# Attention and top-1 experts on one core: the second products of full blocks read the weights in place, at addresses in 16 registers of TensorE, and routing is staged two groups ahead

## The chip, the cores and the metric

One Trainium2 chip, one core of it. The number is the device time of one execution in microseconds (us). The kernel before has run three times: 1196.02, 1198.91 and 1199.16 us, median 1198.91. All inputs lie in HBM when the time starts, and the output has to lie there when it ends.

## The reference, cut

```python
# B, N, C = 4, 5056, 256;  experts E = 8, width F = 1024
qn = q / (norm(q, axis=1) + 1e-06)                  # a norm for each channel, over the tokens
kn = k / (norm(k, axis=1) + 1e-06)
a  = softmax(kn.transpose(0, 2, 1) @ qn / tau)      # 256 x 256 for each batch
x  = (v @ a).reshape(B * N, C)                      # 20224 tokens
logits = x @ w_gate
e, gate = argmax(logits), its softmax probability
out[token] = gate * (relu(x[token] @ w1[e]) @ w2[e])
```

## The kernel before, in words

**Attention.** A batch has 10 groups of 512 tokens (`T` = 4 tiles of 128). SyncE loads the inputs as 128x1024 tiles (`fed`), three ahead of their use (`AHEAD`). For a batch, TensorE multiplies k and q tiles (`sp`, line 226), the softmax gives the matrix `a` (kept as a high and a low half, `a_h` and `a_l`), and `px` (line 396) is v times `a`, together with the router's logits. ScalarE casts each v tile to `hi` (line 192), VectorE makes the remainder `lo` (line 194), and ScalarE also squares and sums tiles by channel for the norms (line 184). ScalarE does its instructions in program order.

**Routing.** For each token VectorE finds the expert and a slot behind the tokens of that expert. ScalarE and VectorE pack the row (`rows`, lines 352 and 353: the token as two float16 parts, its gate factor, its number), and GpSimd writes it to its slot in the DRAM tensor `xs` with an indirect DMA (line 523).

**Experts in blocks.** A block is 256 rows of one expert, read from `xs` by SyncE with a transposing DMA (`xT`, line 699). The float16 parts are multiplied as high*high + high*low + low*high. A full block has 48 products of 128x128x256 for the first matrix (`hp`, line 730) and 48 for the second (`y`, line 756). ScalarE's ReLU (line 738) and VectorE (line 739) make the two halves of the hidden layer, `ht`. All experts' weights stand in SBUF in `W`, 8192 columns of float16 for each expert, but which expert a block has is known only on the chip: VectorE reads the number into a register (line 711) and copies the weights in eight pieces of 128x1024 to buffers `wp` (line 718, `piece`), four for the first matrix and four for the second; `WP` = 5 buffers. TensorE reads only `wp`. ScalarE scales `y` to `o` (line 766), and GpSimd scatters it to `out` (line 769).

**Lists of blocks.** Experts can start on a batch's rows before the last batch is routed. After certain numbers of tokens (`SORTED`) `table(stage)` counts on the chip which 256-row blocks must by now be full, and writes their experts and first rows into a list `c_tb`; SyncE (line 694) and VectorE (line 711) read an entry for each block. `SURE` is the number of full blocks that any data must have by then: 5, 12, 32, 52 and 72. What is left is done in small blocks of 128 rows, 18 of them here, at half the products of a full block. A block's load waits for all scatters of its stage and of those before (`loaded`).

**Order.** The attention of batches 1 to 3 is a side stream, given out between the blocks: `marks` and `amounts` say how much of it (in rough ns of TensorE) must have been issued by which block, linearly in between. A list `coming` sets the order of the loads of `fed`. The batch's list is made behind its tenth group. `EARLY` = 2 ends a batch's side work two blocks ahead of the first block that needs it. A scheduler then orders each engine's instructions by their dependencies and priorities.

Of the kernel before, what the change touches and what calls it, by code (L numbers as in the profile page):

```python
# [20 lines left out]
P = 128  # L21
# [7 lines left out]
G = 10  # L29
# [3 lines left out]
SORTED = [CUT * T * P] + [N * (b + 1) for b in range(B)]  # L33
# [31 lines left out]
def attention_then_experts(ctx, tc, qk, v, wt, chs, kc, out):  # L65
# [97 lines left out]
    WP = 5  # L163
    PT = 2 * T
    EARLY = 2
    PAUSE = -1
# [67 lines left out]
    def rest_of(b, sp, x_split):  # L234
# [107 lines left out]
        pending, packed, slots_of = [], [], {}  # L342

# [13 lines left out]
        def give(g):  # L357
            rows = packed.pop(0)
            z, si = slots_of.pop(g)
            vec.reciprocal(out=rows[:, :, 256], in_=z)  # L360
            for t in range(T):
                n = 64 if g == G - 1 and t == T - 1 else P
                held.append((
                    0 if b == 0 and g < CUT else b + 1, rows, t, si[:, t : t + 1], b * N + (g * T + t) * P, n, b == 0
                ))

        for pair in range(G // 2):
# [5 lines left out]
            for h in range(2):  # L373
                g = 2 * pair + h
                if b == 0:
                    raw = v_cell(g)
                else:
                    raw = fed("v", b, g)
                if x_split:
                    hl = split(raw)  # L380
                xg = work.tile([P, T, C + E], F32, tag="xg", name="xg", bufs=2)
                for t in range(T):
                    if b > 0:
                        px = ps_a.tile([P, C + E], F32, tag=f"p{t % 2}", name="px")
# [30 lines left out]
                if b == 0 or h == 1 or pair > 0:  # L415
                    convert()
                if h == 0 and b > 0 and pair > 0:
# [16 lines left out]
            last = pair == G // 2 - 1  # L434
            if last:
                vec.memset(ex[64:P, :, PT], 0.0)
# [26 lines left out]
            if b == 0 or last:  # L463
# [5 lines left out]
        drip(False, len(held))  # L469
# [60 lines left out]

    written = [[] for _ in range(LAST + 1)]
    SYNC = mybir.DependencyInfo(mybir.DependencyClass.Sync, mybir.DependencyReason.DATA)

    def scattered(stage, ins):
        raw = ins.ins
        for s2 in range(LAST):
# [6 lines left out]
    def loaded(stage, ins):  # L543
# [3 lines left out]
        for s2 in range(stage + 1, LAST):  # L547
# [5 lines left out]
    def padded(ins):  # L553
        raw = ins.ins
        for s2 in range(LAST):
# [20 lines left out]

    def table(stage):
# [6 lines left out]
        whole = work.tile([1, 512], F32, tag=tag, name="c_grid", bufs=bufs)  # L584
        grid = whole[:, 0 : 2 * 24 * E].rearrange("p (a i e) -> p a i e", a=2, e=E)
        square = whole[:, 384:448].rearrange("p (a e) -> p a e", e=E)
# [65 lines left out]
        te_f = tiny.tile([1, 24], F32, name="c_ef", bufs=1)[:, 0:quota]  # L652
        ts_f = tiny.tile([1, 24], F32, name="c_sf", bufs=1)[:, 0:quota]
# [3 lines left out]
        tb = tiny.tile([1, 2, 24], I32, name="c_tb", bufs=3)  # L657
# [5 lines left out]
        if final:  # L663
# [3 lines left out]
            gap = tiny.tile([1, 24], F32, name="c_gap", bufs=1)[:, 0:quota]  # L667
# [24 lines left out]
    def block_load(stage, tab, i):  # L692
        nt = P if stage == LAST else BLK
# [13 lines left out]
    def block(stage, tab, i, xT, mt):  # L707
# [12 lines left out]

        hts = []
        for f in range(8):
# [12 lines left out]
            behind[0] = mm.ins.name  # L735
            if f % nf == nf - 1:
# [98 lines left out]
    vec.tensor_scalar(out=before[0][:, :, 0], in0=e7, scalar1=NPAD / P, scalar2=None, op0=ALU.mult)  # L835
    done = one.tile([1, E], F32, name="done")
# [65 lines left out]
    left, soon = [("k", 2, n) for n in range(half)], list(range(20))  # L902
    steps = 0
    for r in range(1, E):
        for _ in range(6):
            steps += 1
            if steps % 4 == 3 and left:
                coming.append(left.pop(0))
            if steps >= 33:
                coming.append(("c", 2, soon.pop(0)))  # L910
        coming += [("c", 1, n) for n in range(2 * r + 4, 2 * r + 6)]
# [28 lines left out]
    def opening():  # L940
        scores_of(2)
        steps = 0
        for r in range(1, E):
            for _ in range(6):
# [3 lines left out]
                if steps % 4 == 3 and steps < 4 * HALF:  # L948
                    yield next(chunks[2])
                if steps >= 33:  # L950
                    yield next(norms_of[2])
# [4 lines left out]
            take(norms, 2)  # L956

    def rows_of(b):
        at = 0
        for n in rests[b]:  # L960
            yield n
# [9 lines left out]
        tables[b + 1] = yield from table(b + 1)  # L971
        if b == B - 1:
            tables[LAST] = yield from table(LAST)
# [8 lines left out]
    parts = [42 * 1000 + HALF * CHUNK + 10 * 300, 5000 + X_ALL + HALF * CHUNK + 10 * 300]  # L982
    parts += [5000 + X_ALL + nch * CHUNK + 20 * 300, 5000 + X_ALL]
    marks = [0.0, float(SURE[0])] + [SURE[b] - EARLY for b in range(1, B)]
# [70 lines left out]
```

## Time and profile before

| | |
|---|---|
| median of the runs shown | 1198.91 us |
| the profiled execution's own time | 1198.22 us |
| its span in the trace | 1196.4 us |
| TensorE matrix products, busy | 1162.0 us |
| TensorE weight loads, busy (beside the products) | 1026.0 us |
| VectorE / ScalarE / GpSimd, busy | 807.1 / 618.4 / 458.8 us |
| DMA, mean over the span | 148 GB/s |

The span runs from the first to the last instruction; 1.8 us of the execution's own time lie outside it. "Busy" counts an engine's computing instructions only. Each engine also has a sequencer, which takes the instructions in order, and does register work and waits by itself; the views mark its rows with a q (SPq, DVEq, PEldq). A product on TensorE has a weight load ahead of it, which has rows of its own (PEld).

### The profile page before, as it was taken

The numbers are of one execution on the slowest core, as the hardware profiler recorded it, in microseconds if no ns is written. First come the engines' busy times: TensorE is split into PE (matmuls) and PEld (weight loads), VectorE is DVE, ScalarE is ACT, GpSimd is POOL, SyncE is SP. The second block draws the span as 40 slices with busy tenths as digits, with TensorE's granted clock in tenths as the row PEclk, the third lists the DMA queues.
The fourth block names the chain that finished last, engine by engine and source line by source line (L and its number), as shares of the span: only waits on it lengthen the run. The fifth ranks groups of instructions, "written<-read, shape, count | busy, mean of one in ns | idle before, by whom it ended". The sixth has DMA issues, their size and how long they took to land. (4 is left out here: it accounts for less than half of the span.)

```text
span 1196.4 us, 28325 instructions
## 1 busy us (share of the span) xinstructions
PE 1162.0 (97%) x10194; PEld 1026.0 (86%) x10194; DVE 807.1 (67%) x2122; ACT 618.4 (52%) x1385; POOL 458.8 (38%) x724
## 2 busy tenths in 40 slices
PE   9998999899899999999999999999999999999998
PEld 7777879688778888998888988999878888889997
DVE  5575787776686776667687666767665555556886
ACT  6586478697745665666644555555422333223332
POOL 0067812228481343433545145363552222222222
PEclk9999999999899999999999999999999999999999
DMA  9968998958625555565644233222142211211121
GB/s 376 410 259 289 335 379 244 285 180 260 193 92 136 157 163 160 164 174 168 153 118 101 74 83 97 83 76 67 59 119 54 55 50 50 54 44 46 51 50 23
DMA packets 153488, 177.38 MB, mean 148 GB/s; under 512 B 116604, under 2 KB 118017, under 8 KB 151424
## 3 DMA queue, kind: packets, MB, share of 16 engines
q1 hardware_dynamic: 137952, 133.94, 38.6%
q0 software_dynamic: 15392, 41.60, 9.4%
q8 instruction: 81, 1.33, 0.5%
q14 instruction: 63, 0.52, 0.1%
HBM read 111.49 MB, written 43.29 MB: 129 GB/s over the span
## 5 line engine op out<-in xcount | busy, mean ns | idle before, releaser
L756 PE MATMUL y<-wp,ht 128*128 128x256 f16 x3888 | 454.6, 273 | 6.2 <-DVE wp L718 2.9
L730 PE MATMUL hp<-xT,wp 128*128 128x256 f16 (+1 forms) x4320 | 450.9, 262 | 1.6 <-DVE ht L739 1.0
L756 PEld LDWEIGHTS <-ht 128*128 128x128 f16 x3888 | 372.4, 98 | 59.7 <-ACT ht L738 7.2
L730 PEld LDWEIGHTS <-wp 128*128 128x128 f16 x4320 | 383.6, 98 | 46.4 <-issue 2.6
L718 DVE COPY wp<-W 128x1024 f16 (+1 forms) x720 | 291.9, 440 | 184.3 <-PE y L756 139.4
L769 POOL DMA_INDIRECT out<-o,mt x162 | 179.2, 1106 | 465.7 <-ACT o L766 442.1
L738 ACT ACTIVATE ht<-hp 128x512 f16<-128x512 f32 x324 | 192.3, 594 | 171.3 <-PE hp L730 169.5
L739 DVE SCALAR_TENSOR_TENSOR ht<-hp,ht 128x512 f16<-128x512 f32 x324 | 222.4, 687 | 44.3 <-ACT ht L738 41.9
L523 POOL DMA_INDIRECT xs<-rows,r_si x160 | 178.6, 1116 | 138.9 <-ACT rows L352 58.3
L766 ACT ACTIVATE o<-y,b_fac 128x256 f32<-128x256 f32 x162 | 68.8, 469 | 246.0 <-PE y L756 228.3
L513 POOL TENSOR_SCALAR rows<-kt 128x1 int32<-128x1 f32 x160 | 44.9, 281 | 127.0 <-PE sp L226 79.3
L398 ACT COPY xg<-px 128x264 f32<-128x264 f32 x160 | 57.8, 370 | 59.7 <-PE px L396 39.4
L352 ACT ACTIVATE rows<-xg,x_sc 128x256 f16<-128x256 f32 x160 | 71.2, 499 | 23.4 <-issue 8.1
L194 DVE TENSOR_TENSOR lo<-fed,hi 128x1024 fp32r<-128x1024 f32 x50 | 61.8, 1235 | 28.1 <-ACT hi L192 28.1
L353 DVE SCALAR_TENSOR_TENSOR rows<-xg,x_sc,rows 128x256 f16<-128x256 f32 x160 | 71.2, 480 | 13.4 <-ACT rows L352 13.0
L396 PE MATMUL px<-a_h,hi 128*128 128x264 f32 x240 | 73.9, 310 | 5.6 <-ACT hi L192 5.5
L396 PE MATMUL px<-a_h,lo 128*128 128x264 f32 x240 | 68.5, 292 | 0.0
L396 PE MATMUL px<-a_l,hi 128*128 128x264 f32 x240 | 68.5, 288 | 0.0
L400 ACT ACTIVATE xjunk<-xg 128x256 bf16<-128x256 f32 x160 | 66.8, 417 | 2.7
L192 ACT CAST hi<-fed 128x1024 fp32r<-128x1024 f32 x50 | 52.0, 1040 | 24.0 <-PE sp L226 13.2
L184 ACT ACTIVATE fed<-fed 128x1024 f32<-128x1024 f32 x54 | 56.7, 1050 | 13.7 <-DMA fed<-in_by_channel 13.7
L396 PEld LDWEIGHTS px<-a_h,hi 128*128 128x128 f32 x240 | 45.8, 192 | 8.4 <-ACT hi L192 6.9
(161 smaller groups left out, 973.2 us busy)
## 6 DMA issues: line engine op xcount, KB each, us to landing
fed<-in_by_channel SPq DMA_DIRECT2D x54, 512.0 KB, 4.1
fed<-in_qk SPq DMA_DIRECT2D x40, 512.0 KB, 4.6
W<-in_w SPq DMA_DIRECT2D x15, 1024.0 KB, 10.6
fed<-in_v SPq DMA_DIRECT2D x30, 512.0 KB, 4.5
raw<-in_qk SPq DMA_DIRECT2D x20, 512.0 KB, 9.2
W<-in_qk SPq DMA_DIRECT2D x20, 512.0 KB, 10.2
W<-in_v SPq DMA_DIRECT2D x10, 512.0 KB, 11.0
W<-in_by_channel SPq DMA_DIRECT2D x6, 512.0 KB, 10.2
```

Source lines behind the costliest of these rows:

```text
L352: act.activation(r16[:, t, 0:C], x, AF.Copy, scale=by)
L353: vec.scalar_tensor_tensor(out=r16[:, t, C : 2 * C], in0=x, scalar=by, in1=r16[:, t, 0:C], op0=ALU.mult, op1=ALU.subtract)
L396: mm = pe.matmul(px, hl[vh][:, c, ts], ah[:, c, :], start=(n == 0), stop=(n == 5))
L400: act.activation(junk, xg[:, t, 0:C], AF.Square, accum_out=ss[:, h * T + t : h * T + t + 1])
L523: ins = pool.indirect_dma_start(out=xs[:, :], out_offset=bass.IndirectOffsetOnAxis(ap=slot[:n], axis=0), in_=row[:n], in_offset=None)
L718: vec.tensor_copy(out=t, in_=Wf[:, ds(e * 8192 + n * 1024, 1024)])
L730: mm = pe.matmul(hp[:, f % nf, :], wp[:, dc, wh, (f % 2) * P : (f % 2 + 1) * P], xT[:, 2 * xh + dc, :], start=(n == 0), stop=(n == 5),)
L738: evicted.append(act.activation(ht[:, 0], hp, AF.Relu).ins.name)
L739: halved = vec.scalar_tensor_tensor(out=ht[:, 1], in0=hp, scalar=0.0, in1=ht[:, 0], op0=ALU.max, op1=ALU.subtract)
L756: mm = pe.matmul(ys[:, j, :], hts[f // nf][:, hh, f % nf, j * P : (j + 1) * P], wps[f // 2][:, f % 2, wh, :], start=(n == 0), stop=(n == 23),)
L766: act.activation(o, ys[:, j, :], AF.Copy, scale=fac[:, j : j + 1])
L769: ins = pool.indirect_dma_start(out=out[:, :], out_offset=bass.IndirectOffsetOnAxis(ap=mt.bitcast(I32)[:, j, 1:2], axis=0), in_=o, in_offs ...
```

## The change

- **Second products in place.** In all stages but the last (`straight`) the 48 `y` products of a block read `W` itself. VectorE computes 16 column addresses (`b_where`, line 740 of the changed kernel), one instruction on TensorE loads them into 16 registers (line 761), placed among the block's first products, and each `y` product (line 787) takes its address from one of them. The four copies for the second matrix are gone in these blocks; small blocks copy all eight as before. Over the program the copies go from 720 (90 blocks x 8) to 480 (68 x 4 + 26 x 8). `WP` is 4.
- **Stages two groups ahead.** A list is made behind group 8 of a batch's 10 (`TAIL` = 2, `ROUTED`); the last two groups' rows belong to the next stage. `SURE` becomes 5, 12, 28, 48 and 68 full blocks, and 26 small ones follow (94 blocks in place of 90). `EARLY` is 3, `marks` and `parts` follow, and scatters are no longer flushed at a batch's end.
- **Load order.** Three written lists (`opens`) say after which step of the opening a load and its work come, in place of rules.
- **Schedule.** The scheduler orders by estimated durations (`schedule_with_timeline_sim`).

```diff
-SORTED = [CUT * T * P] + [N * (b + 1) for b in range(B)]
+TAIL = 2
+SORTED = [CUT * T * P, N] + [N * b + (G - TAIL) * T * P for b in range(1, B)]
...
-    WP = 5
+    WP = 4
...
-    EARLY = 2
-    PAUSE = -1
+    EARLY = 3
+    TAKES = 6
+    GROUPS = [CUT, G - CUT, G - TAIL] + [G] * (B - 2) + [TAIL]
+    PAUSE, ROUTED = -1, -2
...
+            stage = int(g >= CUT) if b == 0 else b + 1 + (g >= G - TAIL)
...
+            if b > 0 and pair == (G - TAIL) // 2 - 1:
+                yield ROUTED
+        if b == 0:
+            drip(False, len(held))
-        drip(False, len(held))
...
+        straight = stage != LAST
+        if straight:
+            where = tiny.tile([1, 16], I32, name="b_where", bufs=2)
+            vec.scalar_tensor_tensor(
+                out=where, in0=tab[0][0:1, i : i + 1].to_broadcast([1, 16]), scalar=8192.0, in1=pieces_at,
+                op0=ALU.mult, op1=ALU.add,
+            )
...
+            if straight and f == 1:
+                (load,), at = nc.values_load_multi_w_load_instructions(
+                    where, engines=[ENG.PE], min_val=4096, max_val=8192 * (i + 1 if stage == 0 else E) - 256,
+                    skip_runtime_bounds_check_because=WHY, bass_reorder=False,
+                )
+                tc.add_manual_dep(load.ins, mm.ins.name, HERE, reason="among the first products")
...
-                if j == 0 and n < 16 and n % 4 == 0:
+                if not straight and n < 16 and n % 4 == 0:
                     wps.append(piece(4 + f // 2).rearrange("p (f s d) -> p f s d", f=2, s=2))
+                w2 = Wf[:, ds(at[2 * f + wh], C)] if straight else wps[f // 2][:, f % 2, wh, :]
                 mm = pe.matmul(
-                    ys[:, j, :], hts[f // nf][:, hh, f % nf, j * P : (j + 1) * P], wps[f // 2][:, f % 2, wh, :],
+                    ys[:, j, :], hts[f // nf][:, hh, f % nf, j * P : (j + 1) * P], w2,
...
-    with tile.TileContext(nc) as tc:
+    with tile.TileContext(nc, schedule_with_timeline_sim=True) as tc:
```

**On TensorE, where a late full block's first products meet second products.** Before, a pair is a weight load and a product, for both kinds (`ht` and `wp` ahead of the arrow are the two operands):

```order
L730 LDWEIGHTS wp
L730 MATMUL hp<-xT,wp 128x256
L756 LDWEIGHTS ht
L756 MATMUL y<-wp,ht 128x256
L756 LDWEIGHTS ht
L756 MATMUL y<-wp,ht 128x256
```

The same place now (`ISA` is a register instruction, here multiply and add, which makes the address of the product behind it):

```order
L754 LDWEIGHTS wp
L754 MATMUL hp<-xT,wp 128x256
L761 TENSOR_LOAD b_where
L787 LDWEIGHTS ht
L787 ISA
L787 MATMUL y<-W,ht 128x256
L787 LDWEIGHTS ht
L787 ISA
L787 MATMUL y<-W,ht 128x256
```

There are 68 such loads of 16 registers and 3264 register instructions, 48 for each full block, where there were none. In the late blocks the first 12 of a block's second products stand among the next block's first 12 first products; the next block's load of registers comes behind these, then the other 36 second products in one piece, then the next block's other 36 first products. Before, 48 and 48 stood in one piece each.

**On VectorE, at a late full block.** Before (`b_fac` is the block's gate factor, `ISA` the copy's address):

```order
L746 TENSOR_SCALAR b_fac<-mt,fe 128x2
L718 ISA
L718 COPY wp<-W 128x1024
L718 ISA
L718 COPY wp<-W 128x1024
L718 ISA
L718 COPY wp<-W 128x1024
L718 ISA
L718 COPY wp<-W 128x1024
L718 ISA
L718 COPY wp<-W 128x1024
L739 SCALAR_TENSOR_TENSOR ht<-hp,ht 128x512
```

Now:

```order
L776 TENSOR_SCALAR b_fac<-mt,fe 128x2
L740 SCALAR_TENSOR_TENSOR b_where<-c_tb,pieces_at 1x16
L727 TENSOR_LOAD c_tb
L734 ISA
L734 COPY wp<-W 128x1024
L769 SCALAR_TENSOR_TENSOR ht<-hp,ht 128x512
L734 ISA
L734 COPY wp<-W 128x1024
L769 SCALAR_TENSOR_TENSOR ht<-hp,ht 128x512
```

Five copies in a row ahead of an `ht` became one; the block's addresses are made at its start.

**On VectorE, where the list of the stage behind the third batch (batch 2) is finished.** Before, the list (`c_tb` of `c_sf`, the first rows) comes behind all ten groups, and copies of the blocks follow it:

```order
L655 TENSOR_REDUCE c_sf<-c_grid 1x20
L656 SCALAR_TENSOR_TENSOR c_sf<-kt,c_sf 1x20
L718 ISA
L718 COPY wp<-W 128x1024
L684 TENSOR_SCALAR c_tb<-c_sf 1x20
L718 ISA
L718 COPY wp<-W 128x1024
```

The same list now:

```order
L664 TENSOR_TENSOR c_grid<-c_grid,c_fs 1x160
L669 TENSOR_REDUCE c_sf<-c_grid 1x20
L670 SCALAR_TENSOR_TENSOR c_sf<-kt,c_sf 1x20
L197 TENSOR_TENSOR lo<-fed,hi 128x1024
L698 TENSOR_SCALAR c_tb<-c_sf 1x20
```

A dozen rows on, still within one block's work, the routing of the batch's remaining groups begins (`r_m`, `x_sc`, `r_d`; `rows` packs tokens):

```order
L776 TENSOR_SCALAR b_fac<-mt,fe 128x2
L197 TENSOR_TENSOR lo<-fed,hi 128x1024
L426 TENSOR_REDUCE r_m<-xg 128x4
L416 TENSOR_SCALAR x_sc<-x_ss 128x4
L427 TENSOR_TENSOR r_d<-xg,r_m 128x32
L357 SCALAR_TENSOR_TENSOR rows<-xg,x_sc,rows 128x256 x4
L740 SCALAR_TENSOR_TENSOR b_where<-c_tb,pieces_at 1x16
```

The list stands ahead of two groups' routing that stood ahead of it before.

## Rows read from the trace of the kernel before

**Rows 1.** The page: the span, and the busy time of TensorE and VectorE (share of the span, instructions).

```profile
span 1196.4 us, 28325 instructions
PE 1162.0 (97%) x10194; PEld 1026.0 (86%) x10194; DVE 807.1 (67%) x2122; ACT 618.4 (52%) x1385; POOL 458.8 (38%) x724
```

**Rows 2.** Busy time of each engine by stretches of the span. Columns: from and to, length, busy us (instructions) of PE, PEld, DVE, ACT and POOL, the granted TensorE clock as a share, mean DMA share, GB/s.

```profile
120.00:320.00 200.00, 190.14 (x1571) 163.78 (x1570) 146.94 (x395) 143.89 (x311) 87.65 (x131) 0.99 0.85 270
320.00:360.00 40.00, 34.84 (x283) 29.76 (x283) 30.57 (x113) 18.02 (x47) 27.61 (x47) 0.96 0.37 124
360.00:600.00 240.00, 238.16 (x2087) 212.46 (x2086) 159.43 (x358) 143.93 (x321) 89.49 (x133) 1.00 0.59 160
600.00:640.00 40.00, 38.80 (x343) 33.83 (x342) 34.10 (x118) 17.37 (x38) 22.03 (x39) 1.00 0.37 110
640.00:840.00 200.00, 199.70 (x1800) 180.51 (x1799) 136.83 (x334) 105.87 (x260) 86.18 (x127) 1.00 0.30 82
840.00:920.00 80.00, 77.84 (x705) 68.35 (x704) 52.88 (x175) 27.03 (x57) 36.23 (x61) 1.00 0.30 80
920.00:1090.00 170.00, 170.00 (x1560) 152.38 (x1558) 95.41 (x212) 52.51 (x99) 39.93 (x66) 1.00 0.20 50
1090.00:1196.40 106.40, 101.25 (x1342) 93.28 (x1340) 79.63 (x200) 31.30 (x57) 27.15 (x39) 1.00 0.17 42
...
280.00:320.00 40.00, 36.76 (x281) 32.94 (x280) 25.81 (x75) 28.90 (x81) 27.50 (x43) 0.96 0.70 211
```

**Rows 3.** The chain of work that ended last, in order of time: start, us, what. There are 19 such rows, one for each full block; the first and the last.

```profile
899.36 7.61 issue
...
1088.00 7.60 issue
```

**Rows 4.** Timeline of TensorE at the small blocks: start, us (the records of products overlap), engine, line, operation, count. The first products of the first small block, and of the 18th and last.

```profile
1094.84 2.84 PE L730 MATMUL hp<-xT,wp 128*128 128x128 f16 x48
...
1185.74 2.84 PE L730 MATMUL hp<-xT,wp 128*128 128x128 f16 x48
```

**Rows 5.** What TensorE waited for from 120 to 360 us, and (last row) from 840 to 920: us in total, times, the longest.

```profile
PE px L396 <- ACT hi L192: 5.5, 2, 3.2
...
PE y L756 <- DVE ht L739: 1.2, 1, 1.2
...
PE y L756 <- DVE wp L718: 1.0, 1, 1.0
...
PE y L756 <- DVE wp L718: 1.5, 3, 0.8
```

**Rows 6.** What the DMA queue of SyncE waited for: us in total, times, the longest.

```profile
SPq L699 <- DMA xs<-rows,r_si: 37.8, 6, 17.5
...
SPq L694 <- DVE wp L718: 18.1, 1, 18.1
SPq L694 <- DVE c_tb L684: 16.9, 1, 16.9
```

**Rows 7.** Timeline of ScalarE and then of TensorE at two places: start, us, line, operation, count, and in brackets the idle time before it and what ended that.

```profile
298.99 1.06 ACT L184 ACTIVATE fed<-fed 128x1024 f32<-128x1024 f32 x1 [3.22 <-DMA fed<-in_by_channel]
...
321.73 1.06 ACT L184 ACTIVATE fed<-fed 128x1024 f32<-128x1024 f32 x1 [2.06 <-DMA fed<-in_by_channel]
...
302.08 0.44 PE L396 MATMUL px<-a_h,hi 128*128 128x264 f32 x1 [3.24 <-ACT hi L192]
302.31 0.42 PE L396 MATMUL px<-a_l,hi 128*128 128x264 f32 x1
...
324.81 0.39 PE L396 MATMUL px<-a_h,hi 128*128 128x264 f32 x1 [2.25 <-ACT hi L192]
325.04 0.28 PE L396 MATMUL px<-a_l,hi 128*128 128x264 f32 x1
```

**Rows 8.** VectorE's copies among the costliest groups (count, busy us and mean ns of one, idle time before them), and four of them in the timeline.

```profile
L718 DVE COPY wp<-W 128x1024 f16 (+1 forms) x720 | 291.9, 440 | 184.3 <-PE y L756 139.4
...
905.74 1.43 DVE L718 COPY wp<-W 128x1024 f16 x4 [3.07 <-PE y L756]
```

**Rows 9.** The loads of one word into one register, by line: engine's sequencer, count, duration in ns as least/median/most, first and last start in us.

```profile
L711 DVEq TENSOR_LOAD <-c_tb x89: 299/304/703, 137.9 to 1182.8; - x89
...
L694 SPq TENSOR_LOAD <-c_tb x90: 262/277/468, 93.5 to 1169.1; - x90
...
L1012 PEldq TENSOR_LOAD <-nb x1: 489/489/489, 1190.1 to 1190.1; - x1
```

**Rows 10.** Register instructions (`FUSED_REGOPS`), a cheap semaphore instruction, and VectorE's small `b_fac`, columns as in rows 9. The last row is TensorE's sequencer, at 870.0 us.

```profile
L718 DVEq EVENT_SEMAPHORE  x423: 21/21/21, 203.5 to 1188.1; - x141
...
L746 DVE TENSOR_SCALAR b_fac<-mt,fe x90: 198/219/364, 138.5 to 1189.9; 128x2 f32<-128x2 f32 x72, 128x1 f32<-128x1 f32 x18
L746 DVEq FUSED_REGOPS  x89: 53/53/53, 157.8 to 1189.3; - x89
...
L730 PEldq EVENT_SEMAPHORE  x1: 51/51/51, 870.0 to 870.0; - x1
```

**Rows 11.** Timeline of TensorE: the first products that stand behind that semaphore instruction, and at another place products of 64 columns on ready operands.

```profile
871.92 1.25 PE L730 MATMUL hp<-xT,wp 128*128 128x256 f16 x10
...
290.37 0.20 PE L449 MATMUL rtp<-r_ex,tri 128*128 128x64 f16 x1
290.40 0.20 PE L451 MATMUL rtp<-r_to,ones 128*128 128x64 f16 x1
```

More of the change, by code (lines that the diff above doesn't have):

```diff
@@ L342, in rest_of @@
         pending, packed, slots_of = [], [], {}
+        starts = (0, (G - TAIL) // 2)
         def convert():
@@ L363, in give @@
                 held.append((
-                    0 if b == 0 and g < CUT else b + 1, rows, t, si[:, t : t + 1], b * N + (g * T + t) * P, n, b == 0
+                    stage, rows, t, si[:, t : t + 1], b * N + (g * T + t) * P, n, b == 0
                 ))
@@ L414, in rest_of @@
                 pending.append((xg, sc[:, hs]))
-                if b == 0 or h == 1 or pair > 0:
+                if b == 0 or h == 1 or pair not in starts:
                     convert()
-                if h == 0 and b > 0 and pair > 0:
+                if h == 0 and b > 0 and pair not in starts:
                     give(2 * pair - 1)
@@ L434, in rest_of @@
             last = pair == G // 2 - 1
+            ends = last or pair + 1 in starts
             if last:
@@ L462, in rest_of @@
             give(2 * pair)
-            if b == 0 or last:
+            if b == 0 or ends:
                 if pending:
@@ L535, in scattered @@
         raw = ins.ins
-        for s2 in range(LAST):
+        for s2 in range(LAST + 1):
             tc.declare_no_dep(raw, group=f"scatter{s2}", reason="slots differ")
@@ L546, in loaded @@
             tc.declare_no_dep(raw, group="pads", reason="behind the tokens")
-        for s2 in range(stage + 1, LAST):
+        for s2 in range(stage + 1, LAST + 1):
             tc.declare_no_dep(raw, group=f"scatter{s2}", reason="blocks read are full already")
@@ L554, in padded @@
         raw = ins.ins
-        for s2 in range(LAST):
+        for s2 in range(LAST + 1):
             tc.declare_no_dep(raw, group=f"scatter{s2}", reason="behind the tokens")
@@ L583, in table @@
         tag, bufs = ("hl", 2) if stage else ("wp", WP)
-        whole = work.tile([1, 512], F32, tag=tag, name="c_grid", bufs=bufs)
-        grid = whole[:, 0 : 2 * 24 * E].rearrange("p (a i e) -> p a i e", a=2, e=E)
-        square = whole[:, 384:448].rearrange("p (a e) -> p a e", e=E)
+        most = MOST if stage else 24
+        whole = work.tile([1, 2 * most * E + 128], F32, tag=tag, name="c_grid", bufs=bufs)
+        grid = whole[:, 0 : 2 * most * E].rearrange("p (a i e) -> p a i e", a=2, e=E)
+        square = whole[:, 2 * most * E : 2 * most * E + 64].rearrange("p (a e) -> p a e", e=E)
         sq8 = [1, E, E]
@@ L656, in table @@
         vec.scalar_tensor_tensor(out=ts_f, in0=io, scalar=float(unit), in1=ts_f, op0=ALU.mult, op1=ALU.add)
-        tb = tiny.tile([1, 2, 24], I32, name="c_tb", bufs=3)
+        tb = tiny.tile([1, 2, MOST], I32, name="c_tb", bufs=3)
         tb_e, tb_s = tb[:, 0, :], tb[:, 1, :]
@@ L666, in table @@
             void = g1[:, :, E - 1]
[L667 removed]
+            gap = tiny.tile([1, MOST], F32, name="c_gap", bufs=1)[:, 0:quota]
             vec.tensor_scalar(out=gap, in0=ts_f, scalar1=-1.0, scalar2=float(E * NPAD), op0=ALU.mult, op1=ALU.add)
@@ L692, in block_load @@
     def block_load(stage, tab, i):
+        assert given[: stage + 1] == GROUPS[: stage + 1], (stage, given)
+        assert not any(h[0] <= stage for h in held), stage
         nt = P if stage == LAST else BLK
@@ L835, in attention_then_experts @@
     vec.tensor_scalar(out=before[0][:, :, 0], in0=e7, scalar1=NPAD / P, scalar2=None, op0=ALU.mult)
+    pieces_at = one.tile([1, 16], F32, name="pieces_at")
+    vec.tensor_scalar(
+        out=pieces_at, in0=kt[0:1, K_IOTA + 16 : K_IOTA + 32], scalar1=256.0, scalar2=None, op0=ALU.mult
+    )
     done = one.tile([1, E], F32, name="done")
@@ L901, in attention_then_experts @@
     half = nch // 2
[L902 to L911, printed above, removed]
+    soon = list(range(20))
+    opens = {}
+    for kind, b, first, at in (("c", 1, 6, [9, 12, 15, 18, 20, 22, 24, 26, 28, 30, 32, 34, 36, 38]), ("k", 2, 0, [12, 15, 18, 21, 24, 27, 30, 33, 36, 39]), ("c", 2, 0, [33, 34, 35, 36, 37, 38, 39, 40, 41, 42])):
+        for n, step in enumerate(at):
+            opens.setdefault(step, []).append((kind, b, first + n))
+    for step in range(1, 6 * (E - 1) + 1):
+        coming += opens.get(step, [])
+    soon = soon[10:]
     beside = {}
@@ L947, in opening @@
                 yield 1000
[L948 to L951, printed above, removed]
+                for kind, b, _ in opens.get(steps, []):
+                    yield next(chunks[2] if kind == "k" else norms_of[b])
             if r == 1:
@@ L960, in rows_of @@
         for n in rests[b]:
+            if n == ROUTED:
+                tables[b + 1] = yield from table(b + 1)
+                continue
             yield n
@@ L970, in rows_of @@
                 at += 1
-        tables[b + 1] = yield from table(b + 1)
         if b == B - 1:
+            while held:
+                yield PAUSE
             tables[LAST] = yield from table(LAST)
```

18 lines of the change are left out of this document (12 added, 6 removed).

## The prediction, as it was put on record

> **What bounds the kernel now.** I read the page first: TensorE computes for 1162.0 of a span of 1196.4 us, VectorE for 807.1 [rows 1]. So 34.4 us of the span at most lie in waits of TensorE, and everything else is products, which the change leaves nearly as many as they were. Next the stretches [rows 2]. There the idle time is what the length leaves over the busy time of PE: 9.9 us in 120 to 320, 5.2 in 320 to 360, 1.8 in 360 to 600, 1.2 in 600 to 640, 0.3 in 640 to 840, 2.2 in 840 to 920, none in 920 to 1090. The first 120 us and the last 106 hold the rest, an opening and a drain that the change keeps in kind. What can be gained in between is thus 20.5 us, however many copies go. The chain of waits agrees: from 899 to 1088 us it shows one row per full block that waits for nothing, 18 steps in 188.64 us, 10.48 us each [rows 3], or 109 ns for each of its 96 products. There VectorE is busy 95 of 170 us: faster copies can't speed that stretch.
>
> The short stretches with much idle time are where a stage begins. SyncE's queue shows why: the block loads waited 37.8 us in six places for scatters of rows to `xs`, and the entries of new lists waited 18.1 and 16.9 us for VectorE [rows 6]. TensorE's waits name the other large thing: 5.5 us in two places for `hi` [rows 5]. The timeline shows ScalarE idle for 3.22 and 2.06 us just before, at the norms' line 184, until a DMA of `fed` lands; `hi` stands behind it in ScalarE's order [rows 7].
>
> **Term A, stages two groups ahead.** At 320 to 360, 600 to 640 and 840 to 920 us a stage begins. Without the wait for `hi` at 324.81 (2.25) their idle time is 5.16 - 2.25 = 2.9, 1.2 and 2.2 us, 6.3 together [rows 2, 7]. With the change, the list and the scatters on which the first blocks of a stage wait are done when two groups (two tenths of a batch's routing) are still to come, and VectorE has its list ahead of them, as the order shows. What is late next is the next batch's last two groups, and nothing reads them before the following list. I take 5.5 of 6.3; the bounds are 0 and 6.3.
>
> **Term B, the load order.** The two waits for `hi` are 3.24 and 2.25 us [rows 7], and 280 to 320 and 320 to 360 us have a granted clock of 0.96 where all the neighbours have 0.99 or 1.00 [rows 2]: 4% of 40 us is 1.6 us, twice, 3.2 us. Right behind the first wait a product takes 0.42 us, behind the second 0.28 [rows 7], so the lower of the two clock levels follows idle time here. Together 8.7 us hang on two loads that come late. The written lists move norm loads, and the scheduler places ScalarE's norm by its estimate of when the load lands. But ScalarE still takes its work in order and the DMA share before 320 us is 0.85 [rows 2], so a load can be late at another place. Bounds 0 (the wait moves) and 8.7; I take half, 4.5.
>
> **Term C, VectorE's load.** 240 copies go. One takes 0.440 us busy in the mean, or, four in a row with their addresses, 1.43 / 4 = 0.36 [rows 8]: 86 us of VectorE's 807. Added are 68 tiny instructions for the addresses; the nearest row, `b_fac`, has 0.219 us [rows 10], so 15 us, and off the path while VectorE is 56% busy late and 73% early [rows 2]. Of the idle time that A and B don't hold, 6.6 + 1.8 + 0.3 = 8.7 us between 120 and 840, the rows name VectorE for some 2 to 3 (`ht` 1.2, `wp` 1.0) [rows 5]. I take 1.5; bounds 0 and 3.
>
> **Term D, smaller blocks.** Four full blocks become eight small ones. A small block takes (1185.74 - 1094.84) / 17 = 5.35 us [rows 4], a full one 10.48: 8 x 5.35 - 4 x 10.48 = +0.9. `WP` 4 instead of 5 matters there most, where all eight copies stay: the cover is VectorE's 25% of free time (79.6 busy of 106.4 [rows 2]). If it is gone, a copy's 0.44 us per block would show, 26 x 0.44 = 11 us. I take 0, since four copies take 1.43 us and a half block's first products 2.8 [rows 4, 8].
>
> **Term E, registers on TensorE's sequencer.** No trace row has this. The lead of the sequencer over the products bounds what it can lose: its semaphore instruction at 870.0 us belongs to a product that starts at 871.92 [rows 10, 11], so it runs 1.92 us ahead, some 17 products of 109 ns. A load of registers costs nothing until it takes longer than that. One word takes 0.489 us on this sequencer, 0.277 and 0.304 on SyncE's and VectorE's [rows 9]. Sixteen in one instruction lie between 0.49 (one word's time for all) and 16 x 0.277 = 4.4 us (one after another). Nearest is the one-word row, since it is the same instruction on the same engine, on consecutive words; with each further register at 51 ns, the sequencer's own cheap instruction [rows 10], it is 0.49 + 15 x 0.051 = 1.25 us. That leaves 1.92 - 1.25 = 0.67 us of lead. Then 36 products in a row need an address each. VectorE's sequencer takes 53 ns for an instruction of that kind [rows 10], and a weight load with its product passes the sequencer in 30 ns at most (products 30 ns apart [rows 11]): 83 ns, under 109, so the lead grows again and E is 0. Upper bound: TensorE's semaphore instruction takes 51 ns where VectorE's takes 21 [rows 10]; scaled by that, 53 becomes 129, with the 30 it is 159 ns.
>
> The row of one word on this engine is 0.489 us, and nothing in it tells how 16 go. The Trainium skill, "Runtime: NRT & Kernel Launch", section "Instruction fetch mechanics", says that register loads cost about 200 ns a register even in bulk. By that rule, as an estimate, 16 registers take 3.2 us, 1.3 over the lead, 87 us over 68 blocks, and the change would end near 1275. The one-word rows are above 200 ns, which neither bears it out nor speaks against it for many words.
>
> **The sum.** Against the profiled execution's own 1198.2 us: 1198.2 - 5.5 - 4.5 - 1.5 + 0.9 + 0 = 1187.6, say 1188. That execution lies 0.7 under the median of the runs shown, which is within their spread of 3 us. A difference under 0.3%, 3.6 us, I count as no change. The likeliest case's own range: with all bounds in favour 1198.2 - 6.3 - 8.7 - 3 + 0.9 = 1181, and some 3 less where the new order takes other idle time too, 1178; with A at 3 and the others at 0, 1196; so 1178 to 1196.
>
> **Rivals.**
> 1. *The load of 16 registers outlasts the lead* (slower). Each of the 68 full blocks then stops TensorE by what the load takes beyond 1.92 us. The break-even lies where that loss eats A to C: 10.6 / 68 = 0.16 us, a load of 2.1 us. At 4.4 us: 2.5 x 68 = 168, so 1188 + 168 = 1356; halfway between 2.1 and 4.4, at 3.2, about 1275. For it: the one-word load costs 0.28 to 0.49, and no row tells that this is not paid for every word. Against it: it is one instruction.
> 2. *An address and a product together outlast a product* (slower). Behind a load of 1.25 us, 36 products at d ns use up 0.67 us of lead once d is above 109 + 19 = 128. At the upper bound of 159: 36 x 0.050 - 0.67 = 1.1 us a block, 77 us in all, about 1265. Against it: 53 ns is what the same kind takes on another sequencer.
> 3. *The waits only move* (no change). Stage ends wait for the routing of group 8 now instead of group 10, which must be issued earlier and so crowds VectorE and ScalarE where they are busiest, 73% and 72% in 120 to 320 us [rows 2]; `fed` loads are late at other norms. A, B and C give nothing net: 1198.2 + 0.9 = 1199. For it: the waits of SyncE on VectorE for `c_tb` and `wp` show that the stage ends hang on VectorE's order as well as on scatters. Against it: 86 us of VectorE go.
>
> **How the numbers follow.** Likeliest 0.55, rival 1 0.18, rival 2 0.13, rival 3 0.14. The predicted time is the likeliest case's 1188. Below 1178 I leave 0.03. Rival 1 at 3.2 us and above ends past 1275, rival 2 at its bound at 1265; a top of 1268 keeps rival 2 and the small overruns of rival 1 and leaves about 0.13 out. Faster by over 0.3% is under 1195.3: nearly all of the likeliest, 0.54, and 0.03 of rival 3. The same: 0.08 of rival 3 and 0.02 beside it, 0.10. Slower: rivals 1 and 2 and the rest of rival 3, 0.33.
>
> **What would show it.** For E: the new line's rows of `TENSOR_LOAD` on PE's sequencer, below 1.9 us, register instructions of about 50 to 70 ns, and the steps of the chain between full blocks at 10.48 us still; rival 1 shows as idle time of TensorE once in each full block, rival 2 as products more than 109 ns apart among the `y` alone. For A: the idle time of the stretches where stages begin near zero, and no long waits of SyncE on `xs`. For B: `hi` gone from TensorE's waits and a clock of 1.00 throughout. For C: 480 copies. For D: small blocks still 5.35 us apart. The prediction fails if either price on TensorE's sequencer is beyond the lead, since 68 blocks multiply it, while the gain can't pass some 20 us.

## The result: half a per cent slower

The changed kernel takes 1203.96 us in the median of nine runs (1200.57 to 1209.86), the kernel before 1198.91 beside it (1196.02 to 1201.41): a ratio of 1.0053, 95% interval 1.0035 to 1.0071. The profiled execution is the fastest of the nine, 1200.57 us, so its trace holds 2.3 us of the 5. The mean granted clock was 0.993 in it and 0.988 to 0.995 over the nine; before, 0.997 in the profiled one. The page now:

```profile
span 1198.7 us, 31676 instructions
PE 1155.7 (96%) x10386; PEld 1028.4 (86%) x10386; DVE 721.6 (60%) x1955; ACT 622.9 (52%) x1385; POOL 457.0 (38%) x703
```

VectorE lost 85.5 us of work [rows 1], and the time did not fall. The stretches of the changed kernel, with the columns of [rows 2]:

```profile
120.00:320.00 200.00, 182.72 (x1548) 159.34 (x1549) 134.57 (x378) 146.52 (x314) 79.95 (x114) 1.00 0.83 263
320.00:360.00 40.00, 32.31 (x254) 28.04 (x252) 27.12 (x109) 26.54 (x76) 28.85 (x42) 0.96 0.45 146
360.00:600.00 240.00, 237.65 (x2092) 214.37 (x2090) 143.61 (x362) 146.01 (x334) 106.01 (x157) 0.99 0.59 165
600.00:640.00 40.00, 40.00 (x364) 35.99 (x362) 27.04 (x79) 19.21 (x41) 10.39 (x17) 1.00 0.37 100
640.00:840.00 200.00, 200.00 (x1809) 181.01 (x1808) 116.07 (x320) 105.43 (x258) 95.62 (x144) 1.00 0.33 87
840.00:920.00 80.00, 79.85 (x729) 71.14 (x727) 43.72 (x126) 28.50 (x60) 30.54 (x48) 1.00 0.30 75
...
80.00:120.00 40.00, 35.94 (x186) 30.78 (x185) 18.13 (x94) 18.61 (x61) 33.61 (x69) 0.96 0.51 188
360.00:400.00 40.00, 40.00 (x347) 35.47 (x345) 25.25 (x69) 21.86 (x59) 20.50 (x33) 0.96 0.46 112
560.00:600.00 40.00, 37.65 (x319) 33.12 (x317) 23.03 (x67) 20.15 (x46) 19.14 (x28) 0.96 0.50 146
```

TensorE's idle time from 600 to 920 us went from 3.7 to 0.15: the late stage ends are clean. From 120 to 360 us it went the other way, from 15.0 [rows 2] to 25.0 us. Since the records of products overlap, I also counted every product at the median spacing that its shape has in the trace before, and took that sum from the length of each stretch. The difference of this lost time, after less before:

| stretch, us | 0-120 | 120-200 | 200-280 | 280-400 | 400-600 | 600-920 | 920-end |
|---|---|---|---|---|---|---|---|
| changed less before, us | -3.9 | +8.6 | +0.1 | +3.7 | -3.4 | -5.8 | +2.4 |

With 0.6 us more of products this is the 2.3 us between the spans. So 12 us are lost between 120 and 400, and 10.7 won in the rest (13.1 in three stretches, less 2.4 at the end). Of the 12, 9.7 are idle time (25.0 us now, 15.3 before, where 360 to 400 us had 0.3). The clock is not in the 12: two stretches of 40 us there are at 0.96 now, 320 to 360 and 360 to 400, as two were before, 280 to 320 and 320 to 360 [rows 2].

**The registers cost nothing in the late full blocks.** The new rows on TensorE's sequencer (durations in ns, least/median/most), and the steps of the chain at the late full blocks:

```profile
L761 PEldq TENSOR_LOAD <-b_where x68: 1102/1107/1772, 133.4 to 1037.0; - x68
...
L787 PEldq FUSED_REGOPS  x3264: 37/37/42, 136.3 to 1052.0; - x192
...
941.67 7.60 issue
...
1035.99 7.61 issue
```

Sixteen registers take 1.11 us, under the lead of 1.92, an address 37 ns, and the blocks still stand (1035.99 - 941.67) / 9 = 10.48 us apart. In the whole trace only 1.0 us of TensorE's idle time ahead of a `y` product has no wait to its name, in two places after 600 us, so the trace shows no more than that as a price of the loads elsewhere.

**What TensorE waits for early.** Its waits from 120 to 400 us in the changed kernel (us, times, longest), and ScalarE's there:

```profile
PE y L787 <- ACT o L797: 4.7, 3, 2.2
PE sp L229 <- DMA fed<-in_qk: 4.7, 4, 1.7
PE px L402 <- ACT xg L404: 3.1, 2, 2.1
PE hp L754 <- ACT xg L404: 1.7, 1, 1.7
...
PE px L402 <- ACT hi L195: 1.2, 1, 1.2
...
ACT o L797 <- DMA out<-o,mt: 12.7, 6, 3.4
```

The waits for `hi` fell from 5.5 us [rows 5] to 1.2 here, and other names stand in their place. The rows of `o`, `fed` and `xg` shown here are 14.2 us together; before, TensorE waited 2.2 us for `fed` from 120 to 400 us and for `o` and `xg` in no place that the trace names. One such place, on GpSimd, ScalarE and TensorE:

```profile
350.81 1.06 POOL L533 DMA_INDIRECT xs<-rows,r_si  x1 [0.28 <-POOL rows L523]
...
352.41 1.79 POOL L533 DMA_INDIRECT xs<-rows,r_si  x1 [0.28 <-POOL rows L523]
...
354.60 1.22 POOL L800 DMA_INDIRECT out<-o,mt  x1 [0.17 <-ACT rows L356]
...
357.88 0.47 ACT L797 ACTIVATE o<-y,b_fac 128x256 f32<-128x256 f32 x1 [2.39 <-DMA out<-o,mt]
358.26 0.37 ACT L404 COPY xg<-px 128x264 f32<-128x264 f32 x1
...
358.68 0.39 PE L402 MATMUL px<-a_h,hi 128*128 128x264 f32 x1 [2.13 <-ACT xg L404]
```

GpSimd scatters rows to `xs`, 1.6 us apart, ahead of a scatter of `o` to `out`. ScalarE wants to write the next `o` and has to wait until a buffer of `o` has been read. Behind it in ScalarE's order stands the eviction of `px` to `xg`, and TensorE stands still for 2.13 us for that. This looked like a single cause; the experiments below say that it is not.

### The profile page after: what moved, and what is told of

Read it like the earlier page. It is cut to its first block, busy times and chain, and to the rows that moved or that the text cites. A ratio compares the mean times of both kernels' runs of the same rounds, so it can differ in the third digit from the quotient of the medians.

```text
span 1198.7 us, 31676 instructions
## 1 busy us (share of the span) xinstructions
PE 1155.7 (96%) x10386; PEld 1028.4 (86%) x10386; DVE 721.6 (60%) x1955; ACT 622.9 (52%) x1385; POOL 457.0 (38%) x703
## 4 chain that ended last, share of the span: by engine, by line
PE 50%; issue 23%; POOL 12%; DMA 9%; ACT 3%; DVE 2%; SPq 1%; POOLq 1%; ACTq 0%; DVEq 0%
PE y L787 19%; PE hp L754 18%; POOL out L800 6%; PE px L402 5%; PE sp L229 5%; POOL xs L533 4%; DMA out<-o,mt 2%; DMA raw<-in_qk 2%; PE px L399 2%; DMA W<-in_w 1%; POOL idle L798 1%; POOL rows L523 1%; DMA fed<-in_qk 1%; DMA W<-in_qk 1%; PE gram L133 1%
## 5 line engine op out<-in xcount | busy, mean ns | idle before, releaser
L754 PE MATMUL hp<-xT,wp 128*128 128x256 f16 (+1 forms) x4512 | 471.7, 258 | 3.6 <-ACT xg L404 1.7
L787 PE MATMUL y<-W,ht 128*128 x3264 | 403.3, 275 | 6.2 <-ACT o L797 4.7
L800 POOL DMA_INDIRECT out<-o,mt x162 | 175.2, 1081 | 457.5 <-ACT o L797 428.7
L734 DVE COPY wp<-W 128x1024 f16 (+1 forms) x480 | 198.5, 436 | 105.5 <-PE hp L754 79.4
L523 POOL TENSOR_SCALAR rows<-kt 128x1 int32<-128x1 f32 x160 | 52.2, 326 | 118.4 <-PE sp L229 68.9
L356 ACT ACTIVATE rows<-xg,x_sc 128x256 f16<-128x256 f32 x160 | 68.5, 498 | 16.4 <-issue 8.2
L787 PE MATMUL y<-wp,ht 128*128 128x256 f16 x624 | 73.9, 273 | 1.0 <-issue 0.8
```

What stands on the lines that cost most here:

```text
L356: act.activation(r16[:, t, 0:C], x, AF.Copy, scale=by)
L734: vec.tensor_copy(out=t, in_=Wf[:, ds(e * 8192 + n * 1024, 1024)])
L754: mm = pe.matmul(hp[:, f % nf, :], wp[:, dc, wh, (f % 2) * P : (f % 2 + 1) * P], xT[:, 2 * xh + dc, :], start=(n == 0), stop=(n == 5),)
L787: mm = pe.matmul(ys[:, j, :], hts[f // nf][:, hh, f % nf, j * P : (j + 1) * P], w2, start=(n == 0), stop=(n == 23),)
L800: ins = pool.indirect_dma_start(out=out[:, :], out_offset=bass.IndirectOffsetOnAxis(ap=mt.bitcast(I32)[:, j, 1:2], axis=0), in_=o, in_offs ...
```

## Experiments

All ratios and times are medians of four or more runs beside the kernel before on the same chip. Its own median was 1196.8 in the first group, 1198.8, 1199.5, 1198.8 and 1199.4 in the others.

### One part undone from the changed kernel

Copies back, the scheduler's old order, the old stages, or the old load rules:

```diff
-        straight = stage != LAST
+        straight = False                      # a_no_inplace, with WP = 5 and the copies of the kernel before
...
-    with tile.TileContext(nc, schedule_with_timeline_sim=True) as tc:
+    with tile.TileContext(nc) as tc:          # a_no_durations
...
-TAIL = 2
+TAIL = 0                                      # a_no_stages, with EARLY = 2 and the scatters flushed at a batch's end
...
-    opens = {}                                # a_no_lists: the loops of the kernel before in place of opens
```

> The changed kernel with the second matrix copied again (four copies more in each full block, five wp buffers, no register loads on TensorE); stages, load order and schedule as changed. Theory 1 (the in-place part costs the time: VectorE's b_where waits 49.6 us in 31 places for TensorE's register load, and what stands behind it on VectorE is late): below 1196 us, and the lost time between 120 and 400 us falls by some 10 us. Theory 2 (another part costs it, in-place gains little or some): 1203 to 1212 us, above the changed kernel or level with it, and VectorE back at about 800 us busy.

> The changed kernel with the scheduler ordering as before (no estimated durations). Theory 3 (the order by durations puts TensorE's work of 120 to 400 us behind ScalarE's and VectorE's in-order queues): 1188 to 1194 us, with the waits of y for o gone and idle time of TensorE from 120 to 400 us near 15 us in place of 25. If the schedule is not the cause: within 4 us of 1204, or slower.

> The changed kernel with lists behind group 10 again (SURE 5, 12, 32, 52, 72, 18 small blocks, EARLY 2). Theory 4 (the earlier deadlines crowd batch 1's attention into fewer blocks and cost the 10 us early): 1194 to 1198 us, early idle time near 15 us, but the idle time at 600 to 640 and 840 to 920 us back at 1 to 3 us each. If stages are not the cause: 1206 to 1210 us, since their gain at the late stage ends (about 6 us) is lost.

> The changed kernel with the load order by the old rules. Theory 5 (the written lists bring loads of fed late: TensorE waited 4.7 us for in_qk and 4.1 us for the weights of in_w): 1194 to 1199 us. If the lists are not the cause: within 4 us of 1204.

Measured: 1215.1, 1216.5, 1219.5 and 1207.8 us (ratios 1.0159, 1.0163, 1.0187, 1.0092, each within 0.0018). None of the theories 1, 3, 4 and 5 stands: without any one of the parts the kernel is slower still. The ranges for "not the cause" were too low for in-place products (to 1212) and for stages (to 1210). Each over the kernel before of its own group, the parts gain 6 to 18 us in the others' presence, though together they lose 5.

### One part alone in the kernel before

The same edits from the other side: each of these is the changed kernel with the other three parts undone. No run has all four undone.

> The kernel before with the in-place second products alone (16 registers, four copies fewer per full block, four wp buffers); old stages, lists and schedule. Each of the four parts undone by itself made the changed kernel slower, by 4 to 15 us, so a cost must lie in a part taken alone or in a pair. If the in-place part is free of cost, as its register rows say: 1193 to 1199 us. If it needs the other parts (VectorE's b_where holds back what stands behind it in the old order): 1205 to 1220 us.

> The kernel before with the schedule by estimated durations alone. If this schedule is the part that costs, and the written lists and stages earn it back: 1210 to 1225 us, with the loss between 120 and 400 us. If it is of use by itself: under 1197 us.

> The kernel before with the lists two groups ahead alone. If the earlier deadlines cost in the early stretch what the late stage ends give back: 1196 to 1204 us. If they are what costs when the rest is as before: 1205 to 1215 us. If term A of the prediction stands by itself: 1191 to 1193 us.

> The kernel before with the written load lists alone. Within 4 us of 1197 if the order of loads matters little, as its removal from the changed kernel suggests (4 us); 1201 to 1210 us if the lists fit only the new schedule.

Measured: 1222.0, 1232.9, 1202.4 and 1202.0 us (1.0194, 1.0285, 1.0034, 1.0034, each within 0.0018). Two parts are costly alone, and both end above the ranges that were given for a loss (to 1220 and to 1225 us). The long waits in their traces differ.

*In-place products alone, +23 us.* ScalarE and TensorE in this kernel, then both in the kernel before at the same place:

```profile
161.32 1.15 ACT L151 ACTIVATE W<-W,scales 128x1024 f16<-128x1024 f32 x1 [0.81 <-DVE W L152]
165.97 1.06 ACT L187 ACTIVATE fed<-fed 128x1024 f32<-128x1024 f32 x1 [3.50 <-DMA fed<-in_by_channel]
...
168.30 0.82 ACT L796 ACTIVATE o<-y,b_fac 128x256 f32<-128x256 f32 x2
169.01 1.14 ACT L151 ACTIVATE W<-W,scales 128x1024 f16<-128x1024 f32 x1
170.05 0.59 ACT L767 ACTIVATE ht<-hp 128x512 f16<-128x512 f32 x1
...
168.53 3.67 PE L229 MATMUL sp<-fed 128*128 128x256 f32 x8 [5.60 <-DMA fed<-in_qk]
```

```profile
163.03 0.82 ACT L766 ACTIVATE o<-y,b_fac 128x256 f32<-128x256 f32 x2
163.74 1.15 ACT L150 ACTIVATE W<-W,scales 128x1024 f16<-128x1024 f32 x1
164.78 0.59 ACT L738 ACTIVATE ht<-hp 128x512 f16<-128x512 f32 x1
166.30 1.06 ACT L184 ACTIVATE fed<-fed 128x1024 f32<-128x1024 f32 x1 [0.93 <-DMA fed<-in_by_channel]
...
169.55 1.89 PE L226 MATMUL sp<-fed 128*128 128x256 f32 x8
```

The norm's tile lands near 166 us in both. Before, ScalarE did `o`, a weight piece and `ht` first, and waited 0.93 us. Now the norm stands ahead of these three, which wait with it for 3.5 us, and TensorE has a score product next, 5.60 us before its tile has landed. Before, TensorE came to that product a microsecond later and did not wait. In the stretches 160 to 200 and 200 to 240 us the granted clock is 0.91 and 0.87, where before it was 1.00 in both (this kernel, then the kernel before):

```profile
160.00:200.00 40.00, 34.40 (x305) 30.08 (x303) 26.30 (x53) 27.05 (x42) 7.39 (x8) 0.91 0.78 259
200.00:240.00 40.00, 31.03 (x245) 25.79 (x244) 23.77 (x58) 28.44 (x47) 6.30 (x8) 0.87 0.85 260
```

```profile
160.00:200.00 40.00, 38.97 (x357) 34.20 (x356) 32.06 (x68) 32.21 (x48) 7.72 (x8) 1.00 0.96 312
200.00:240.00 40.00, 36.55 (x301) 29.73 (x300) 29.75 (x77) 28.05 (x52) 11.19 (x13) 1.00 0.87 262
```

That is 40 x 0.09 = 3.6 and 40 x 0.13 = 5.2 us of TensorE's time, by estimate, beside 10.1 us more idle time. The second stretch has another long wait, 5.3 us for `soft` at 230 us, whose cause was not followed. By the count of products, 14 of the 24 us between the two spans lie from 120 to 280 us; the others are spread over the rest. The register loads are no slower here (72 of 1.10 us in the median, 1.45 at most). That the missing copies are what lets the norm come ahead of `o` is a reading of the two orders, not a test.

*Durations alone, +34 us.* TensorE's wait for blocks, SyncE's wait for the list ahead of the first of them, and three stretches:

```profile
PE hp L753 <- DMA xT<-xs: 13.5, 3, 5.4
...
SPq L709 <- DVE c_tb L697: 27.7, 1, 27.7
...
360.00:400.00 40.00, 27.56 (x213) 22.94 (x212) 20.86 (x67) 11.49 (x29) 20.35 (x35) 0.79 0.36 83
640.00:680.00 40.00, 35.44 (x296) 30.58 (x294) 25.72 (x77) 14.91 (x35) 18.33 (x31) 0.91 0.37 82
880.00:920.00 40.00, 35.35 (x309) 30.45 (x308) 29.04 (x110) 10.82 (x22) 23.03 (x41) 0.96 0.36 103
```

At three stage ends the first products wait 4 to 5 us for their block; the trace before names no such wait of TensorE anywhere. Ahead of the first, from 340 to 380 us, SyncE's queue stood 27.7 us for the list and 3.4 us more for scatters of rows. The clock is lower in each of the three stretches; in the first, TensorE also waits 7.0 us for `soft` ahead of the block.

### Buffers for the new waits

```diff
-            o = work.tile([P, C], F32, tag="o", name="o", bufs=2)
+            o = work.tile([P, C], F32, tag="o", name="o", bufs=4)                         # c_o_four; 3 in c_o_three_where_six
...
-            where = tiny.tile([1, 16], I32, name="b_where", bufs=2)
+            where = tiny.tile([1, 16], I32, name="b_where", bufs=6)                       # c_where_six, c_o_three_where_six
```

> The changed kernel with four buffers for o in place of two (room for them by giving r_sl the buffer of r_eq). In the changed kernel ScalarE waited 26.5 us in 13 places, 12.7 of them between 120 and 400 us, to write o until a scatter to out had read the buffer, and TensorE waited 4.7 us for o and 5.9 for xg behind it. Theory A (this queue behind GpSimd's scatters is what the early stretch loses): those waits are gone and the time is 1190 to 1198 us. Theory B (the early loss is spread over the in-order queues and o is one name among others): the waits for o go, others come, within 3 us of 1204.

> The changed kernel with six buffers for b_where in place of two, so that VectorE need not wait until TensorE has loaded the addresses of the block before last. In the changed kernel VectorE waited 49.6 us in 31 places for that, 12.8 of them in 6 places between 120 and 400 us. Theory C (that new wait holds back VectorE's in-order queue and so the early stretch): 1194 to 1199 us. If it only stands where VectorE had nothing due: within 3 us of 1204.

> The changed kernel with three buffers for o and six for b_where. If theories A and C both hold: under 1194 us. If A alone: 1196 to 1201, since one more buffer takes only a part of the waits. If neither: 1202 to 1206.

> The kernel before with the in-place second products alone and five wp buffers (b_only_inplace had four). If the fifth buffer that had to go is what costs the in-place part its 23 us: 1193 to 1201 us. If not, but the order of the work that follows from the missing copies: 1215 to 1225 us.

Measured: 1208.0, 1203.9, 1213.7 and 1221.4 us (1.0071, 1.0045, 1.0120, 1.0174). Theories A and C fall, and so does the fifth `wp` buffer; the third kernel lies above all three of its ranges. With four buffers (made room for by one shared buffer of `r_eq` and `r_sl`, a change of its own) ScalarE's wait for the scatters is 7.1 us instead of 26.5 over the span, as it should be, and another wait is there (the first row is the changed kernel's; the profiled execution with four buffers took 1214.87 us, the slowest of its six):

```profile
ACT o L797 <- DMA out<-o,mt: 26.5, 13, 3.4
...
ACT o L797 <- DMA out<-o,mt: 7.1, 6, 2.2
...
PE hp L754 <- DMA xT<-xs: 7.6, 2, 4.1
```

A buffer more can also give the scheduler another order. Compared place by place, by line and operands without buffer numbers, the traces have another product than the changed kernel's at 2259 of TensorE's 10386 places with four buffers for `o`, and at 1317 in the third kernel. There a wait can't be taken out with all else held. Two runs come near to it: six buffers for `b_where` change 206 places, the fifth `wp` buffer 4 (of 10194, beside in-place products alone), and neither time differs by more than the noise. The six buffers took only part of that wait away, though, from 49.6 to 31.8 us. So these runs show that less of either wait, with the order that comes of it, does not bring the time back.

### Half the weight loads, and the opening's pace

```diff
-                sync.dma_start(out=raw, in_=wt[ds(at, 1), w].rearrange("o p x -> (o p) x"))
+                sync.dma_start(out=raw[:, 0:1024], in_=wt[ds(at, 1), w, :, 0:1024].rearrange("o p x -> (o p) x"))
...
-    marks = [0.0, float(SURE[0])] + ...
+    marks = [0.0, float(SURE[0]) - 0.5] + ...        # h_open alone
```

> The kernel before, but of 15 of the 16 weight matrices only the first half of the columns is loaded (the rest is left as it stands in SBUF), some 7.5 MB less between 80 and 210 us; all computing instructions stay. This is the base for the next two. If loads bind there: 1188 to 1196 us. If not: 1196 to 1200 us.

> The same half loads in the kernel before with in-place second products alone (four wp buffers). Full loads gave 1222, 23 us over before. Theory L (the loads bound 120 to 280 us, and the new order reaches tiles before they land): the difference to h_before falls under 12 us. Theory E (the order among the engines costs it): it stays over 16 us.

> The same half loads in the changed kernel. Full loads gave 1204, 5 us over before. Theory L: faster than h_before by 2 us or more, about 1186 to 1192 us. Theory E: still 3 us or more above h_before.

> The changed kernel, full loads, with six b_where buffers and the opening's side work due half a block earlier. If the pace of the opening is what the new order misses: 1195 to 1200 us. If not: 1202 to 1210 us.

Measured: 1199.4, 1218.5, 1203.6 and 1207.5 us (0.9998, 1.0160, 1.0033, 1.0069). The DMA share of 120 to 200 us fell from 0.99 to 0.83 in the kernel before and from 0.99 to 0.82 in the changed one, and no time moved by more than 4 us. Differences of 19 and 4 us stay where 23 and 5 were: by its ranges theory L falls. Theory E stands as what is left over. The loads have a small share in the in-place kernel: TensorE's waits for the score tiles are 4.4 us there with half the loads, 7.0 with all. The tile of the wait of 5.60 us was not asked for late either; its transfer is issued as early as in the kernel before (first row this kernel, with all loads, second row before):

```profile
154.58 0.33 SPq L492 DMA_DIRECT2D fed<-in_qk  x1
...
155.05 0.33 SPq L483 DMA_DIRECT2D fed<-in_qk  x1
```

So in that place it is TensorE's order that reaches the product too soon. The opening's pace is not it either: 1207.5 us, beside 1203.9 with the six buffers alone.

### Pairs

> The kernel before with the schedule by durations and the lists two groups ahead; copies and load rules as before. Durations alone gave 1233 us, with 13.5 us of waits of hp for xT at three stage ends and a lower clock behind them. If the stages take that back: 1212 to 1221 us with no wait for xT over 1 us. If the stage ends are not what durations cost: above 1226 us.

> The kernel before with in-place second products and the schedule by durations; stages and load rules as before. If in-place products gain under the schedule by durations, as their removal from the changed kernel says (11 us): 1218 to 1226 us, below durations alone (1233). If their costs add (23 and 34 us): above 1245 us.

Measured: 1216.3 and 1231.9 us (1.0148, 1.0278). Stages take half the cost of durations back, and the wait for `xT` is gone from TensorE's named waits. The second kernel lies between its two ranges. The three stretches with durations and stages:

```profile
360.00:400.00 40.00, 37.62 (x319) 33.13 (x320) 26.13 (x72) 20.29 (x56) 22.17 (x35) 0.96 0.45 118
640.00:680.00 40.00, 40.00 (x362) 36.13 (x360) 27.63 (x71) 18.72 (x47) 20.84 (x29) 1.00 0.38 104
880.00:920.00 40.00, 39.41 (x364) 35.09 (x363) 26.00 (x78) 11.61 (x22) 15.68 (x23) 1.00 0.31 78
```

The in-place products' 23 us do not add to the 34 of durations: under that order they change nothing that is clear of the noise (1.0278 beside 1.0285), with stages too they are worth 6 us (1.0148 to 1.0092), with the lists as well 13. All kernels in one table, as us over the kernel before of the same group (i in place, d durations, s stages, l lists):

| i | d | s | l | d s | i d | d s l | i s l | i d l | i d s | i d s l |
|---|---|---|---|---|---|---|---|---|---|---|
| +23 | +34 | +4 | +3 | +17 | +33 | +18 | +20 | +23 | +11 | +5 |

## Why the prediction was wrong

**Read right.** The bound: products fill the time, and what can be won is some 20 us of idle time. *Term E*: 1.25 us forecast for the load, 1.11 measured; 83 ns for an address with its product, and the 37 ns of the address alone are under the 53 assumed; rivals 1 and 2 did not come, and the blocks kept 10.48 us. The Trainium skill's 200 ns a register ("Runtime: NRT & Kernel Launch", "Instruction fetch mechanics") does not hold for this load, 1107 / 16 = 69 ns; the section has the loads in view that the runtime puts in, and this one reads a tile that VectorE wrote. *Term C's* cut of VectorE's work came, by somewhat other sizes: 86 less 15 = 71 us net was forecast and 85.5 measured. The copies gave 93.4 (291.9 [rows 8] to 198.5), and the addresses cost 68 x 0.161 = 10.9:

```profile
L734 DVE COPY wp<-W 128x1024 f16 (+1 forms) x480 | 198.5, 436 | 105.5 <-PE hp L754 79.4 <-PE y L787 14.5 <-issue 7.8
...
L740 DVE SCALAR_TENSOR_TENSOR b_where<-c_tb,pieces_at x68: 132/161/182, 107.1 to 1017.1; 1x16 int32<-1x16 int32 x68
```

**Term A half right.** At 600 to 640 and 840 to 920 us it won 3.2 of 3.4 us. At 320 to 360 us it lost: 7.7 us idle instead of 5.2. SyncE's waits for scatters to `xs` did not go away as the term's sign wanted; they fell from 37.8 us (17.5 the longest) to 31.1 (10.2). And the size was not that of the kernel before: with the old order stages alone cost 4 us, while under the order by durations they are worth 17, since that order makes the stage ends late.

**Terms B and C failed.** The waits for `hi` did shrink, from 5.5 to 1.2 us early, with a new one of 2.4 us from 560 to 600 us; that step is half right. What failed is what came of it: B and C took idle time out of a pool, 4.5 and 1.5 us, as if the rest of the order stood still. The order of every engine was made anew, and between 120 and 400 us, where ScalarE and VectorE are busiest, it lost 12 us at other names (`o`, `xg`, `fed`). I had this as rival 3, put its net at zero and its chance at 0.14. Nothing kept that rival at zero: a new order can be worse, and durations and in-place products, each taken alone, were worse by 34 and 23 us. The "against" that I gave it, 86 us less work on VectorE, did not bear on it. The time came out where that rival had it, within some us; but nothing shows its first reason, that group 8's routing crowds the early stretch, and stages alone cost only 4 us.

**Term D**: the small blocks stand 5.39 us apart instead of 5.35 (twelve steps of the chain from 1120.23 to 1184.90). Over 26 blocks that would be 1.0 us, on top of the 0.9 that was forecast.

**Clock.** Term B counted 3.2 us that the clock would give back, and the sum had nothing for waits that could arise. Of the 3.2 nothing came: where 280 to 360 us was at 0.96, 320 to 400 us is now. 80 to 120 and 560 to 600 us (4.1 and 2.35 idle) are at 0.96 as well, where before they were at 1.00: by estimate 1.6 us each. A lower clock stands in these stretches together with waits, and so it does in those of the experiments, but not each wait brings one: 120 to 200 us of the changed kernel has 8.3 us of idle time at a clock of 1.00.

What stays open: which instruction order on ScalarE and VectorE would keep the late gain and not lose the early 12 us. I have shown single places (`o` behind `out` in the changed kernel, the norm ahead of `o` in the in-place kernel), not that their sum is the 12 us. That the order as a whole is the cause is what is left when the parts, two buffers, the loads and the opening's pace have each failed as a single cause. One run changes the order and keeps the work of the kernel before, the schedule by durations alone, and it shows that an order by itself can cost 34 us; for the 5 us of the changed kernel it stays argued. Of the 5 us in the medians the trace has 2.3; the other runs have a granted clock down to 0.988, and which waits they have in addition no trace shows.

## What to carry to other kernels

Where a scheduler orders in-order queues, an edit's price can lie in the order that it makes more than in the work that it takes away: 86 us less on VectorE gained nothing here. Do each part of a large change alone and undo each from the whole; here both gave losses everywhere (3 to 34 us and 6 to 18), which tells that the parts fit one another and not the kernel before. Forecast a reordering with its own term, of either sign, as wide as the idle time in the stretches where two or more engines are busy.

## What the hardware showed that was not expected

One load of 16 registers on TensorE's sequencer took 1.107 us, where one of a single word took 0.489 [rows 9]: by estimate (1107 - 489) / 15 = 41 ns for each further word. A register instruction of multiply and add took 37 ns there, less than on VectorE's sequencer (53 [rows 10]), although a semaphore instruction takes longer (51 against 21), so scaling one by the other misled the upper bound of the forecast.
